# Relu and square of score tiles by single banks in half-sized buffers, with GpSimd ordered behind planned two-input DVE work and with measured durations in the plan

## Chip, cores and metric

One core of a Trainium2 chip. The metric is the device time of one execution in microseconds (us); a profile's span is 1.7 to 2.0 us shorter than the time of the same execution. Kernels are compared by runs taken in alternation on one chip. All profiles here are of state fast (the two with a single timed run: unknown), with a mean granted TensorE clock of 0.985 to 1.0.

## The reference

Attention with the square of relu in place of softmax, then a two-layer network with the same activation:

```python
scores = (q @ k.transpose(0, 1, 3, 2)) / sqrt(64)          # q, k, v: 8 x 12 x 448 x 64, fp32
attn = np.maximum(scores, 0.0) ** 2 / 448
x = (attn @ v).transpose(0, 2, 1, 3).reshape(3584, 768)
r = np.maximum(x @ w_in, 0.0)                               # w_in: 768 x 2048
out = (r * r) @ w_out                                       # w_out: 2048 x 768
```

## The kernel before

The kernel is planned before it is emitted: operations are added with their dependencies, buffers, due times and, for some, several engines to choose from; a list scheduler with a table of durations fixes engine, order and buffer of each, and then all are emitted in that order. So a change of a duration or of a buffer re-plans everything after it.

A score tile is two PSUM banks of 448 columns. Each bank is scaled and cut at zero by DVE or ACT into half of a wide fp32 buffer, and one instruction squares both halves, on ACT or GpSimd:

```python
"rel": fixed(sb, "rel", 4, [P, 1024], FP32),
...
first = [plan.add([dve(width, ...), act(width, ...)], [op], [sp[e], r], due=plan.now + 0.2)
         for e in range(2)]
second = plan.add([
    act(n, lambda: nc.scalar.activation(out=dst(), in_=rel(), func=AF.Square)),
    ("POOL", 0.0018 * n + 0.05, 0.0018 * n + 0.08,
     lambda: nc.gpsimd.tensor_mul(dst(), rel(), rel()))],
    first, [r, at], due=plan.now + 4.0)               # n = 2 * width
```

The output side multiplies sums of activations (and of the weights `w_out`) to save matmuls. These sums ("combinations") are two-input fp16 operations on DVE; the plan starts one only when GpSimd is free, or adds GpSimd's rest to its duration:

```python
st[name] = plan.add([("DVE", 0.6, 0.68, emit, 0, True)], deps, [buf] + srcs), buf
```

The emitted program had no order between the two engines there. GpSimd also issues the loads that cast to fp16, among them those of `v`, which the plan held as one operation of two transfers:

```python
for r in range(2):
    hs = slice(1, 3) if r else slice(0, 4, 3)
    nc.gpsimd.dma_start(out=buf.tile[64 * r:64 * r + 64], in_=src[:, u, hs])
```

In the first 45 us, where PE has nothing to do in the plan, filler matmuls are emitted.

## Time and profile before

| | before |
|---|---|
| time, median of 3 runs | 383.37 us (383.33 to 383.42) |
| the profiled run, and its span | 384.0 us, 382.0 us |
| PE busy | 371.8 us, 97% |
| DVE, ACT, GpSimd busy | 268.5, 272.0, 191.0 us |

The lines of the profile that carry the argument stand in the prediction; a line of a group gives operation, shapes and count, then busy us and mean ns of one, then the idle time before them and what ended it.

### The profile page before, as it was taken

The page shows a single profiled execution, that of the slowest core. Times are in us where ns is not written, and L with a number is a line of the kernel's source. Part 1 is how long each engine was busy: PE and PEld are TensorE (multiplying, and loading weights), DVE is VectorE, ACT ScalarE, POOL GpSimd, SP SyncE. Part 2 cuts the span into 40 slices and gives each one's busy share as a digit, 9 for nine tenths or more (in the row PEclk, how much of TensorE's full clock was granted, in tenths as well). Part 3 has the DMA queues.
Part 4 walks back from the last instruction along what each step waited for, and adds up shares of the span by engine and source line. Part 5 has one row for each costly group of instructions (what it writes and reads, how often), then busy time and mean ns, then how long its engine had stood idle before and what let it go on. Part 6 is the DMA issues. An engine that isn't in the chain of part 4 may idle for free.

```text
span 382.0 us, 8653 instructions
## 1 busy us (share of the span) xinstructions
PE 371.8 (97%) x3283; PEld 197.9 (52%) x3283; DVE 268.5 (70%) x464; ACT 272.0 (71%) x500; POOL 191.0 (50%) x184
## 2 busy tenths in 40 slices
PE   7799999999999999999999999999999999999995
PEld 3445565544465445544554555545555545555553
DVE  2976889687975677687996575885886768256731
ACT  4998999699877788687876786786794784244221
POOL 7987768383726665565564554664641333001000
PEclk9989999999999999999999999999999999999999
DMA  8999998987278966559369664674553002300243
GB/s 179 194 208 198 195 225 221 247 194 167 48 184 190 159 177 135 120 142 206 79 127 218 159 169 73 180 170 94 129 105 82 2 1 54 73 21 0 61 106 82
DMA packets 70216, 51.34 MB, mean 134 GB/s; under 512 B 36896, under 2 KB 70176, under 8 KB 70176
## 3 DMA queue, kind: packets, MB, share of 16 engines
q1 hardware_dynamic: 52384, 35.86, 38.2%
q0 software_dynamic: 16928, 14.09, 24.6%
q10 hardware_dynamic: 864, 0.85, 0.6%
q8 instruction: 25, 0.41, 0.4%
q14 instruction: 15, 0.12, 0.1%
HBM read 45.61 MB, written 11.01 MB: 148 GB/s over the span
## 4 chain that ended last, share of the span: by engine, by line
PE 92%; ACT 2%; DMA 2%; DVE 1%; POOL 1%; issue 1%; POOLq 0%; ACTq 0%
PE mm L632 38%; PE mm L846 31%; PE mm L505 10%; PE mm L570 8%; PE mm L781 3%; DMA g<-in_q_dram 2%; PE mm L681 2%; PE mm L444 1%; ACT comb L539 1%; DVE comb L825 1%; ACT rel L535 0%; POOL at L541 0%; DVE g L616 0%; ACT at L539 0%; PE mm L708 0%
## 5 line engine op out<-in xcount | busy, mean ns | idle before, releaser
L632 PE MATMUL mm<-xt,w 128*128 128x448 f16 (+1 forms) x768 | 149.0, 346 | 0.1
L541 POOL TENSOR_TENSOR at<-rel 128x896 f16<-128x896 f32 (+1 forms) x63 | 102.2, 1626 | 92.5 <-DVE rel L532 76.5
L616 DVE SCALAR_TENSOR_TENSOR g<-mm,g 128x448 f16<-128x448 f32 (+1 forms) x128 | 77.3, 605 | 50.4 <-ACT g L621 48.9
L632 PEld LDWEIGHTS <-w 128*128 128x128 f16 x768 | 72.3, 98 | 70.4 <-issue 11.7
L532 DVE TENSOR_SCALAR rel<-mm 128x448 f32<-128x448 f32 (+2 forms) x172 | 95.6, 596 | 15.7 <-PE mm L505 14.1
L621 ACT ACTIVATE g<-mm 128x448 f16<-128x448 f32 (+1 forms) x128 | 68.4, 539 | 47.2 <-PE mm L632 47.1
L539 ACT ACTIVATE at<-rel 128x896 f16<-128x896 f32 (+1 forms) x105 | 97.7, 948 | 1.1 <-DVE rel L532 0.6
L535 ACT ACTIVATE rel<-mm 128x448 f32<-128x448 f32 (+2 forms) x176 | 84.8, 550 | 2.9 <-PE mm L505 2.7
L846 PEld LDWEIGHTS <-comb 128*128 128x128 f16 x416 | 39.5, 98 | 30.3 <-issue 4.3
L765 ACT ACTIVATE part<-mm 128x384 f32<-128x384 f32 x45 | 22.3, 499 | 44.6 <-PE mm L846 42.3
L505 PE MATMUL mm<-qkt,qkt 64*64 64x448 f16 (+2 forms) x756 | 52.6, 340 | 1.4 <-DVE rel L532 0.3
L424 POOL CAST blk<-raw 128x896 f16<-128x896 f32 x36 | 36.5, 1024 | 23.4 <-DMA raw<-in_k_dram 11.7
L858 DVE SCALAR_TENSOR_TENSOR part<-mm,part 128x384 f32<-128x384 f32 x52 | 28.3, 554 | 24.9 <-ACT part L765 13.8
L846 PE MATMUL mm<-wt,comb 128*128 128x384 f16 x208 | 36.8, 327 | 0.2 <-DVE comb L825 0.2
L846 PE MATMUL mm<-w,comb 128*128 128x384 f16 x208 | 36.7, 327 | 0.0
L846 PEld LDWEIGHTS <-g 128*128 128x128 f16 x264 | 25.3, 98 | 19.1 <-issue 2.7
L570 PE MATMUL mm<-at,vs 64*64 64x448 f16 (+1 forms) x672 | 35.1, 344 | 0.0
L505 PEld LDWEIGHTS <-qkt 64*64 64x64 f16 x756 | 19.1, 106 | 26.2 <-issue 21.4
L474 POOL DMA_DIRECT2D vs<-in_v_dram x48 | 29.8, 631 | 4.2 <-DVE rel L532 2.0
L846 PE MATMUL mm<-w,g 128*128 128x384 f16 x176 | 31.1, 327 | 0.1
L570 PEld LDWEIGHTS <-vs 64*64 64x64 f16 x756 | 22.2, 108 | 14.7 <-issue 4.9
L747 POOL COPY rest<-g 128x1024 f16<-128x1024 f16 x8 | 8.8, 1103 | 40.6 <-DVE g L616 40.6
(61 smaller groups left out, 207.8 us busy)
## 6 DMA issues: line engine op xcount, KB each, us to landing
out_dram<-part SPq DMA_DIRECT2D x108, 96.0 KB, 2.2
raw<-in_k_dram SPq DMA_DIRECT2D x18, 448.0 KB, 4.2
raw<-in_q_dram SPq DMA_DIRECT2D x18, 448.0 KB, 5.0
vs<-in_v_dram POOLq DMA_DIRECT2D x48, 112.0 KB, 4.3
w<-in_moe_w_in_dram POOLq DMA_DIRECT2D x4, 768.0 KB, 11.8
w<-in_moe_w_out_dram POOLq DMA_DIRECT2D x4, 768.0 KB, 13.5
g<-in_k_dram POOLq DMA_DIRECT2D x4, 224.0 KB, 11.4
g<-in_q_dram POOLq DMA_DIRECT2D x4, 224.0 KB, 9.9
```

Of the source, the lines that this page charges most:

```text
L424: return lambda: fn(blk.tile.rearrange("p t (f d) -> p f t d", f=2), tile_of().rearrange("p f (t d) -> p f t d", d=D))
L474: nc.gpsimd.dma_start(out=buf.tile[64 * r:64 * r + 64], in_=src[:, u, hs])
L505: nc.tensor.matmul(sp[e].tile[64 * c:64 * c + 64, c0:c0 + w].rearrange("p (t c) -> p t c", c=TP), lhsT=kT[r, t, 64 * e:64 * e + 64], rhs=q ...
L532: dve(width, lambda e=e: nc.vector.tensor_scalar(out=rel()[:, e], in0=sp[e].tile[:, 0:width], scalar1=0.0, scalar2=SK, op0=ALU.max, op1=AL ...
L535: act(width, lambda e=e: nc.scalar.activation(out=rel()[:, e], in_=sp[e].tile[:, 0:width], func=AF.Relu, scale=SK))],
L539: act(n, lambda: nc.scalar.activation(out=dst(), in_=rel(), func=AF.Square)),
L541: lambda: nc.gpsimd.tensor_mul(dst(), rel(), rel()))],
L570: nc.tensor.matmul(banks[f].tile[64 * e:64 * e + 64, c0:c0 + w], lhsT=vs[r, e ^ c, t * D:(t + 1) * D], rhs=a[r, e, :], start=(t == 0), sto ...
L616: nc.vector.scalar_tensor_tensor(out=dst, in0=src, scalar=0.0, in1=dst, op0=ALU.is_gt, op1=ALU.mult)
L621: nc.scalar.activation(out=dst, in_=src, func=AF.Square)
L632: nc.tensor.matmul(bank.tile[:, c0:c0 + w], lhsT=w1[f // 4][:, m, f % 4 * P:(f % 4 + 1) * P], rhs=xts[b].tile[:, m, cols], start=(m == 0), ...
L846: nc.tensor.matmul(buf.tile[:, 0:HALF], lhsT=lhs()[:, j, :], rhs=w[:, j, :], start=(first and j == 0), stop=(j == NH - 1), skip_group_chec ...
```

## The change

Its intent: a square can start when one bank is ready, buffers come free in halves, the plan's durations are closer to the measured ones, the two transfers of `v` are planned one by one, and GpSimd's compute really waits where the plan had DVE's two-input work go first.

```diff
-        for emit in self.order:
-            emit()
+        alone = None
+        for emit, op in self.order:
+            got = emit()
+            if op is None:
+                continue
+            if len(op.way) > 5:
+                alone = got
+            elif alone is not None and op.engine == "POOL" and not op.size:
+                self.behind(got, alone)
+                alone = None
...
-                            self.sent += [op.end + (0.8 if op.end > 15.0 else 0.0)] * (2 if op.size == 458752 and took > 1.0 else 1)
+                            self.sent.append(op.end + (0.8 if op.end > 15.0 else 0.3))
...
-        "rel": fixed(sb, "rel", 4, [P, 1024], FP32),
+        "rel": fixed(sb, "rel", 8, [P, 512], FP32),
...
-        vst[n] = plan.add([("POOL", 1.25, 1.25, emit, QK)], bufs=[buf], after=after, due=due), buf
+        vst[n] = [plan.add([("POOL", 0.62, 0.62, emit(r), QK // 2)], bufs=[buf], after=after,
+                           due=due) for r in range(2)], buf
...
+        return plan.add([
+            act(width, lambda: nc.scalar.activation(
+                out=dst(), in_=r.tile[:, 0:width], func=AF.Square)),
+            ("POOL", 0.13 + 0.00172 * width, 0.19 + 0.00172 * width,
+             lambda: nc.gpsimd.tensor_mul(dst(), r.tile[:, 0:width], r.tile[:, 0:width]))],
+            [first], [r, at], due=plan.now + 4.0)
```

(`behind` adds a dependency of the GpSimd instruction on the DVE one. Cut: the rest of the new `squared`, and returns of instructions.)

More of the change, by code (lines that the diff above doesn't have):

```diff
@@ L205, in simulate @@
                         busy, took = busy + wait, took + wait
-                    op.engine, op.start = eng, begin
+                    op.engine, op.start, op.way = eng, begin, alt
                     op.end = begin + took
@@ L219, in simulate @@
                             b.tile, b.slot = slot[2], slot[1]
-                    self.order.append(emit)
+                    self.order.append((emit, op))
                     heapq.heappush(events, self.busy[eng])
@@ L259, in fill @@
             slot = min(free)
-            self.order.append(lambda: self.filler(slot[2]))
+            self.order.append((lambda: self.filler(slot[2]), None))
             self.pools["mm"].remove(slot)
@@ L348, with behind @@
     plan.cold = 6.6
+    def behind(later, first):
+        tc.add_manual_dep(
+            later.ins, first.ins.name, mybir.DependencyInfo(
+                mybir.DependencyClass.Sync, mybir.DependencyReason.ANTI), reason="shared port")
+    plan.behind = behind
     def act(n, emit):
@@ L469, in load_v, with emit @@
         src = v[b].rearrange("(u x) (p t) d -> p u x (t d)", x=4, t=TJ)
-        def emit():
-            for r in range(2):
-                hs = slice(1, 3) if r else slice(0, 4, 3)
-                nc.gpsimd.dma_start(out=buf.tile[64 * r:64 * r + 64], in_=src[:, u, hs])
-        vst[n] = plan.add([("POOL", 1.25, 1.25, emit, QK)], bufs=[buf], after=after, due=due), buf
+        def emit(r):
+            hs = slice(1, 3) if r else slice(0, 4, 3)
+            return lambda: nc.gpsimd.dma_start(
+                out=buf.tile[64 * r:64 * r + 64], in_=src[:, u, hs])
+        vst[n] = [plan.add([("POOL", 0.62, 0.62, emit(r), QK // 2)], bufs=[buf], after=after,
+                           due=due) for r in range(2)], buf
     def load_w1(i, after, due=None):
@@ L515, in scores, with squared, dst @@
                        "tile", at)
-    def square(op, sp, width, pool="at"):
-        at, r = Buf(pool), Buf("rel")
-        flat = [2, width]
-        def rel():
-            return r.tile[:, 0:2 * width].rearrange("p (e c) -> p e c", e=2)
-        def dst():
+    def squared(op, bank, width, dst, at):
+        r = Buf("rel")
+        first = plan.add([
+            dve(width, lambda: nc.vector.tensor_scalar(
+                out=r.tile[:, 0:width], in0=bank.tile[:, 0:width], scalar1=0.0, scalar2=SK,
+                op0=ALU.max, op1=ALU.mult)),
+            act(width, lambda: nc.scalar.activation(
+                out=r.tile[:, 0:width], in_=bank.tile[:, 0:width], func=AF.Relu, scale=SK))],
+            [op], [bank, r], due=plan.now + 0.2)
+        return plan.add([
+            act(width, lambda: nc.scalar.activation(
+                out=dst(), in_=r.tile[:, 0:width], func=AF.Square)),
+            ("POOL", 0.13 + 0.00172 * width, 0.19 + 0.00172 * width,
+             lambda: nc.gpsimd.tensor_mul(dst(), r.tile[:, 0:width], r.tile[:, 0:width]))],
+            [first], [r, at], due=plan.now + 4.0)
+    def square(op, sp, width, pool="at"):
+        at = Buf(pool)
+        def dst(e):
             t = at.tile
@@ L527, in dst @@
                 t = t.rearrange("p f c -> p (f c)").rearrange("p (e c) -> p e c", e=2)
-            return t[:, :, 0:width]
-        n = 2 * width
-        first = [plan.add([
-            dve(width, lambda e=e: nc.vector.tensor_scalar(
-                out=rel()[:, e], in0=sp[e].tile[:, 0:width], scalar1=0.0, scalar2=SK,
-                op0=ALU.max, op1=ALU.mult)),
-            act(width, lambda e=e: nc.scalar.activation(
-                out=rel()[:, e], in_=sp[e].tile[:, 0:width], func=AF.Relu, scale=SK))],
-            [op], [sp[e], r], due=plan.now + 0.2) for e in range(2)]
-        second = plan.add([
-            act(n, lambda: nc.scalar.activation(out=dst(), in_=rel(), func=AF.Square)),
-            ("POOL", 0.0018 * n + 0.05, 0.0018 * n + 0.08,
-             lambda: nc.gpsimd.tensor_mul(dst(), rel(), rel()))],
-            first, [r, at], due=plan.now + 4.0)
-        return second, at
+            return t[:, e, 0:width]
+        return [squared(op, sp[e], width, lambda e=e: dst(e), at)
+                for e in range(2)], at
     xts: dict = {}
@@ L576, in av @@
         before = av_ops.get(n, [])[-1:] + (av_ops[n - 1][-1:] if joint else [])
-        op = plan.pe(max(0.1, 0.000437 * w) * len(ts), emit, [z[0] for z in used] + [vst[n][0]] + before,
+        op = plan.pe(max(0.1, 0.000437 * w) * len(ts), emit, [y for z in used for y in z[0]] + vst[n][0] + before,
                      [z[1] for z in used] + [vst[n][1]] + banks, "tile", at)
@@ L746, in emit @@
             def emit(i=i, b=b):
-                nc.gpsimd.tensor_copy(buf.tile[:, :, 64 * i:64 * i + 64],
-                                      gts[b].tile[:, :, 3 * P:S])
+                return nc.gpsimd.tensor_copy(buf.tile[:, :, 64 * i:64 * i + 64],
+                                             gts[b].tile[:, :, 3 * P:S])
             ops.append(plan.add([("POOL", 1.55, 1.6, emit)], g_ops[b], [buf, gts[b]]))
@@ L824, in emit @@
             def emit():
-                fn(buf.tile, x(), y())
+                return fn(buf.tile, x(), y())
             st[name] = plan.add([("DVE", 0.6, 0.68, emit, 0, True)], deps, [buf] + srcs), buf
```

## The prediction

> **What bounds the kernel now.** I read the page first, then busy time by stretch, the waits of the matmul engine, its timeline around the end of the start-up, and the groups by shape. The page's totals and chain:
>
> ```profile
> PE 371.8 (97%) x3283; PEld 197.9 (52%) x3283; DVE 268.5 (70%) x464; ACT 272.0 (71%) x500; POOL 191.0 (50%) x184
> PE 92%; ACT 2%; DMA 2%; DVE 1%; POOL 1%; issue 1%; POOLq 0%; ACTq 0%
> ```
>
> TensorE is busy for 97% of the span and holds 92% of the chain that ended last. Busy time by stretch tells where the rest is:
>
> ```profile
> 10.00:20.00 10.00, 7.62 (x213) 5.07 (x213) 9.12 (x22) 9.89 (x16) 9.46 (x13) 0.95 1.22 196
> 20.00:32.00 12.00, 11.27 (x140) 5.69 (x133) 8.67 (x20) 11.48 (x26) 9.12 (x9) 0.90 1.24 205
> ...
> 100.00:340.00 240.00, 240.00 (x1950) 125.37 (x1948) 172.79 (x290) 172.83 (x317) 117.41 (x102) 1.00 0.54 122
> 340.00:378.00 38.00, 37.60 (x222) 21.36 (x220) 20.64 (x35) 11.27 (x22) 1.56 (x1) 1.00 0.21 50
> ```
>
> The columns after the stretch's length are PE, PEld, DVE, ACT, POOL, then the granted clock, the DMA share and GB/s. From 100 to 340 us PE has no idle time at full clock, while DVE and ACT have 28% to spare. Only before 32 us is it the other way round: ACT is nearly full and PE waits. After 36 us, the waits of PE's matmuls hold one row:
>
> ```profile
> PE mm L846 <- DVE comb L825: 0.2, 1, 0.2
> ```
>
> A wait that the pipeline's modelled ends hide would not show there, so I also compared the spacing of matmul starts with its usual value for the shape. After 36 us I found some 1.3 us of excess in all, the largest 0.33 us at 353.7 us. So the relus and squares are off the path after the start-up.
>
> What ends the start-up is visible in PE's timeline and in the rows of the load of the first weight:
>
> ```profile
> 31.33 0.32 PE L505 MATMUL mm<-qkt,qkt 64*64 64x320 f16 x2 [0.29 <-DVE xt L592]
> 31.84 0.27 PE L991 MATMUL mm<-part 128*128 128x256 f16 x1 [0.19 <-ACT xt L590]
> 31.95 1.46 PE L681 MATMUL mm<-w,xt 128*128 128x512 f16 x6
> ```
>
> ```profile
> L479 POOL DMA_DIRECT2D w<-in_moe_w_in_dram x4: 828/840/887, 10.7 to 14.4; - x4
> ...
> DMA to landing us min/median/max: 8.6/11.8/17.4
> ```
>
> The last quarter of the weight is issued at 14.42 us and takes 17.4 us, the maximum of the row: it lands at 31.83 us. The fourth L681 block, the first to use it, starts at 31.95 us after one filler (L991). I call this start the gate. PE does useful tile work before it, waits and fillers included, but the same matmuls must run after it.
>
> **What the Trainium skill says.** SBUF — State Buffer, section "Who interferes with whom": a DVE operation with two SBUF inputs contends with GpSimd's reads, and the one that issues second fully blocks. The trace agrees: the two-input L825 takes 0.68 us alone, and next to a GpSimd copy it takes 1.52 us (excerpt below); I count 12 of 52 that were stretched, by 8.6 us together, the worst to 2.38 us. TensorEngine Tiling (Array Packing), section "Key Properties": changing the tiling mode drains TensorE. The trace agrees, with the cost worked out below. DMA: Bandwidth & Descriptors, section "SWDGE vs HWDGE vs iDMA": only one context is allocated for DMAs that GpSimd issues, and casts must go there. The trace fits one line of transfers: landings come in issue order, and the DMA share is above 1.2 from 10 to 60 us. GPSIMD Engine Reference, section "3.1 Elementwise — side-by-side cycle accounting": some 2.6 cycles per element for two inputs. Here the slope is smaller, next part.
>
> **The change part by part.** First, squares in halves. Before:
>
> ```profile
> L541 POOL TENSOR_TENSOR at<-rel 128x896 f16<-128x896 f32 x54 | 91.0, 1686 | 91.3 <-DVE rel L532 75.3 <-ACT rel L535 8.5 <-PE mm L570 5.3
> L539 ACT ACTIVATE at<-rel 128x896 f16<-128x896 f32 x93 | 88.9, 973 | 1.0 <-DVE rel L532 0.6 <-ACT g L621 0.2
> L541 POOL TENSOR_TENSOR at<-rel 128x640 f16<-128x640 f32 x9 | 11.2, 1263 | 1.3 <-DVE rel L532 1.2
> L541 POOL TENSOR_TENSOR comb<-rel 128x256 f16<-128x256 f32 x1 | 0.7, 657 | 0.0
> ```
>
> On GpSimd the slope is (1686 - 657) / 640 = 1.61 ns a column (1.9 cycles at the 1.2 GHz of the skill's table), with about 245 ns fixed; 448 columns should take 0.97 us, so two halves cost 1.93 us for 1.69 us. On ACT, 448 columns to fp16 take 0.55 us in another group (the evacuation to xt), two of them 1.10 us for 0.97 us, but the work is about equal because more moves to GpSimd. From the order of the built program: ACT gets 166 halves of 448 where it had 93 wholes, GpSimd 128 where it had 54 wholes, and one of the weight combinations as well. Estimates by engine: GpSimd 128 x 0.97 + 16 x 0.76 + 3 x 1.07 + 0.9 + 3 for the combination = 143 us for 103 us, so 191 goes to about 230 us (60%). ACT 166 x 0.55 + 26 x 0.45 + 7 x 0.60 = 107 us for 103 us, less three relus and three part copies, 3 us: about 273 us. DVE gains those, about 3 us, and loses contention. All of it lies beside PE's 240 us of full work, so on the path it costs about nothing.
>
> Second, GpSimd waits behind DVE's planned two-input work. It takes back most of the 8.6 us of stretch on L825 and 1.2 us on L810: DVE about 262 us. On the path it is worth one place, at the end:
>
> ```profile
> 351.39 0.69 DVE L825 TENSOR_TENSOR comb<-g 128x1024 f16<-128x1024 f16 x1
> 352.00 1.52 DVE L825 TENSOR_TENSOR comb<-g,g 128x1024 f16<-128x1024 f16 x1
> 353.45 0.68 DVE L825 TENSOR_TENSOR comb<-comb,g 128x1024 f16<-128x1024 f16 x1
> ```
>
> ```profile
> 351.42 1.56 POOL L747 COPY rest<-g 128x1024 f16<-128x1024 f16 x1 [30.82 <-DVE g L616]
> ```
>
> The GpSimd copy blocks the second combination by 0.84 us, and PE then waits for the third one, 0.33 us by spacing. With the copy behind, that wait goes: -0.3 us. The copy itself is needed only at 355.1 us.
>
> Third, the measured durations change the order of everything. Counted in the built program, TensorE has the same 2,862 matmuls from the gate on, before and after, but 56 changes from dense to tiled matmuls and 56 back where it had 59 and 59. One pair, from the timeline:
>
> ```profile
> 202.68 0.73 PE L632 MATMUL mm<-xt,w 128*128 128x448 f16 x3
> 203.34 0.57 PE L505 MATMUL mm<-qkt,qkt 64*64 64x448 f16 x8
> 203.85 1.31 PE L632 MATMUL mm<-xt,w 128*128 128x448 f16 x6
> ```
>
> Three dense matmuls at their usual 0.189 us are 0.57 us and took 0.66; eight scores, four at a time at 0.179 us, are 0.36 us and took 0.51. A pair costs about 0.24 us, and three fewer give -0.7 us.
>
> Before the gate the work is the same too, but fillers go from 8 to 20. Fifteen stand in early waits for loads. Five stand just before the gate where there was one, at 0.11 us each. If PE comes there early, they are free; if it comes only when the weight lands, they cost up to 0.4 us. Four scores fewer are left between the third AV burst and the gate, so PE should come earlier; I put +0.2 us. The DMAs issued by GpSimd stay in the same order, with squares among them; the second quarter of the weight was issued 6.5 us before the first one landed (12.73 and 19.28 us), so 1 us of delay there leaves the line full and the gate in place.
>
> New waits from new places of halves I put at +0.3 us, a quarter of the present excess. Sum: -0.7 - 0.3 + 0.2 + 0.3 = -0.5 us; 383.4 becomes 382.9 us.
>
> **The rivals.** (1) The start-up shortens: ACT is 99% busy from 10 to 20 us, halves are ready sooner and GpSimd takes more, so PE could gain 2 to 4 us of its idle time there: 380 to 381 us. For it speaks the chain, which goes through squares between 11 and 19 us; against it the landing at 31.83 us, which no relu moves. (2) GpSimd becomes a bound: its squares come late for AV, as it has 20% more to do and now waits for DVE too. A few waits of 0.3 to 1 us would make 384 to 386 us. Against it speak 76.5 us in which its squares waited for DVE's relus, so it is short of input, not of time. (3) Delayed issues: a square waiting on DVE in GpSimd's order holds back a load and empties the line, so the gate slips by 1 to 2 us: 384 to 385 us. The slack of 6.5 us speaks against it. (4) The landing itself falls differently: the last quarter came 4.94 us after the third where the others were 3.8 us apart. If that goes, up to 1 us is gained.
>
> **Range and chances.** All certain terms are under 1 us; the landing and the new waits give the width, a little more on the slower side for (2) and (3). 8 in 10: 381.6 to 384.2 us. A change of 2% is 7.7 us, and PE idles for only 10.2 us in the whole span (382.0 - 371.8). Faster by over 2%: 0.02; within: 0.96; slower: 0.02.
>
> **What would show it.** Right: the fourth weight block starts at 31.9 to 32.4 us; PE has no idle time from 100 to 340 us; L825 near 0.68 us with few above 1; GpSimd near 230 us; PE's last matmul some 345.1 us after the gate, where it now ends 345.8 us after it (377.8 - 31.95). Wrong: a gate more than 1 us away, which would make rival (1), (3) or (4) the truth; or PE waits for at or rel after 60 us, rival (2).

## The result, and the profile after

The changed kernel took 382.85 us (median of 4, 382.81 to 383.00), the kernel before in the same rounds 383.35 us. The ratio of the fast runs is 0.9989, with a 95% interval of 0.9972 to 1.0006. A ratio here is the mean time of one kernel's fast runs over that of the other's in the same rounds, so it is not quite the ratio of the medians. By this measurement alone the sign is not settled.

Totals and chain of the changed kernel:

```profile
PE 372.0 (98%) x3295; PEld 198.6 (52%) x3295; DVE 267.0 (70%) x468; ACT 269.8 (71%) x584; POOL 221.4 (58%) x270
PE 85%; DMA 9%; POOL 3%; ACT 1%; issue 1%; DVE 0%; DVEq 0%
```

GpSimd has 30 us more to do, and the chain holds DMA for 9%: a part of it now runs through transfers. Busy time by stretch (PE, PEld, DVE, ACT, POOL, clock, DMA share, GB/s), with 60 to 100 us, where PE loses 0.5 us:

```profile
10.00:20.00 10.00, 8.05 (x223) 5.28 (x216) 9.56 (x21) 9.91 (x26) 9.62 (x14) 1.00 1.22 193
20.00:32.00 12.00, 10.99 (x134) 5.72 (x133) 9.93 (x22) 11.96 (x35) 11.94 (x19) 1.00 1.25 206
...
60.00:100.00 40.00, 39.50 (x333) 20.20 (x332) 30.67 (x52) 35.28 (x77) 30.52 (x35) 1.00 0.82 169
100.00:340.00 240.00, 240.00 (x1950) 124.40 (x1949) 170.65 (x293) 170.30 (x364) 135.39 (x155) 1.00 0.55 123
```

The gate, in PE's timeline (L1009 are the fillers, L699 the fourth block of the first weight), and the load's source rows (last issue at 14.2 us, 16.6 us to its landing):

```profile
30.40 0.98 PE L1009 MATMUL mm<-part 128*128 128x256 f16 x5
31.22 1.46 PE L699 MATMUL mm<-w,xt 128*128 128x512 f16 x6
```

```profile
L496 POOL DMA_DIRECT2D w<-in_moe_w_in_dram x4: 826/846/887, 10.3 to 14.2; - x4
...
DMA to landing us min/median/max: 9.1/12.4/16.6
```

The weight landed at 30.84 us by the trace, 1 us earlier than in the profile of before, and the gate came 0.38 us after it, behind fillers. ACT's last evacuation to xt before the gate (L608) ended at 31.06 us; that this, and not the landing, sets the gate here is shown below. The groups of squares:

```profile
L548 POOL TENSOR_TENSOR at<-rel 128x448 f16<-128x448 f32 x128 | 119.1, 949 | 67.6 <-DVE rel L538 50.6 <-ACT rel L541 8.4 <-DVE comb L843 5.8
L545 ACT ACTIVATE at<-rel 128x448 f16<-128x448 f32 x166 | 90.4, 601 | 0.5 <-PE mm L588 0.5
```

DVE and GpSimd near the end, where before a copy stretched a combination to 1.52 us:

```profile
350.81 0.69 DVE L843 TENSOR_TENSOR comb<-g 128x1024 f16<-128x1024 f16 x1
351.42 0.68 DVE L843 TENSOR_TENSOR comb<-g,g 128x1024 f16<-128x1024 f16 x1
352.02 0.68 DVE L843 TENSOR_TENSOR comb<-comb,g 128x1024 f16<-128x1024 f16 x1
```

```profile
352.77 1.04 POOL L765 COPY rest<-g 128x1024 f16<-128x1024 f16 x1 [31.82 <-DVE comb L843]
```

The copy begins behind the third combination and ends PE's wait of before. The waits of PE's matmuls after 36 us:

```profile
PE mm L522 <- DMA qkt<-blk: 0.4, 1, 0.4
PE mm L522 <- DVE rel L538: 0.2, 1, 0.2
```

The first is new: a score at 75.2 us waits for a transposed load of q or k. By the spacing of starts it costs 0.55 us.

Two lengths are used from here on. "Gate lag" is the time from the landing of the last quarter of the first weight to the gate. "After the gate" is the time from the gate to the start of the last matmul; all kernels have the same 2,862 matmuls in it, but for e9 and e10, with three fillers more each, and e11 and e12, with the 16 that were added. "Stall" is the excess of one spacing over its usual value, listed from 55 ns on.

### The profile page after: what moved, and what is told of

Read it like the earlier page. It is cut to its first block, busy times and chain, and to the rows that moved or that the text cites. A ratio compares the mean times of both kernels' runs of the same rounds, so it can differ in the third digit from the quotient of the medians.

```text
span 381.1 us, 8809 instructions
## 1 busy us (share of the span) xinstructions
PE 372.0 (98%) x3295; PEld 198.6 (52%) x3295; DVE 267.0 (70%) x468; ACT 269.8 (71%) x584; POOL 221.4 (58%) x270
## 4 chain that ended last, share of the span: by engine, by line
PE 85%; DMA 9%; POOL 3%; ACT 1%; issue 1%; DVE 0%; DVEq 0%
PE mm L650 34%; PE mm L864 32%; PE mm L522 8%; PE mm L588 7%; DMA w<-in_moe_w_out_dram 5%; DMA vs<-in_v_dram 3%; PE mm L799 2%; POOL at L548 2%; DMA qkt<-blk 2%; PE mm L1006 1%; PE mm L460 1%; POOL g L406 1%; PE mm L1009 1%; ACT rel L541 0%; ACT comb L545 0%
## 5 line engine op out<-in xcount | busy, mean ns | idle before, releaser
L548 POOL TENSOR_TENSOR at<-rel 128x448 f16<-128x448 f32 (+1 forms) x144 | 130.1, 924 | 67.7 <-DVE rel L538 50.6
L538 DVE TENSOR_SCALAR rel<-mm 128x448 f32<-128x448 f32 (+3 forms) x176 | 97.6, 596 | 14.6 <-PE mm L522 13.2
L545 ACT ACTIVATE at<-rel 128x448 f16<-128x448 f32 (+1 forms) x192 | 101.5, 589 | 0.5 <-PE mm L588 0.5
L541 ACT ACTIVATE rel<-mm 128x448 f32<-128x448 f32 (+2 forms) x172 | 83.0, 548 | 5.4 <-PE mm L522 5.1
L783 ACT ACTIVATE part<-mm 128x384 f32<-128x384 f32 x42 | 20.9, 497 | 44.0 <-PE mm L864 43.1
L440 POOL CAST blk<-raw 128x896 f16<-128x896 f32 x36 | 33.5, 945 | 21.8 <-DVE wt L828 5.4
```

The source lines that it names most:

```text
L440: return lambda: fn(blk.tile.rearrange("p t (f d) -> p f t d", f=2), tile_of().rearrange("p f (t d) -> p f t d", d=D))
L538: dve(width, lambda: nc.vector.tensor_scalar(out=r.tile[:, 0:width], in0=bank.tile[:, 0:width], scalar1=0.0, scalar2=SK, op0=ALU.max, op1= ...
L541: act(width, lambda: nc.scalar.activation(out=r.tile[:, 0:width], in_=bank.tile[:, 0:width], func=AF.Relu, scale=SK))],
L545: act(width, lambda: nc.scalar.activation(out=dst(), in_=r.tile[:, 0:width], func=AF.Square)),
L548: lambda: nc.gpsimd.tensor_mul(dst(), r.tile[:, 0:width], r.tile[:, 0:width]))],
```

## The experiments

Twelve kernels ran, in three calls; each call has its own runs of the kernel before (medians 383.32, 382.97 and 383.31 us). There the runs of the kernel before spread over 1.6 to 2.6 us, so intervals are wide, and the lengths from the traces say more than medians. Of the eight ways to combine the change's three parts (halves, split loads, waits), halves with the waits alone was not run.

**e1, control: the kernel before again, no edit.** It asks whether the earlier gate belongs to the change.

> The kernel before, run once more for a second profile. In the two profiles at hand the fourth block of the first weight (the gate) starts at 31.95 us before and at 31.22 us after, because the last quarter of the weight landed at 31.83 and 30.84 us. Theory A (my prediction: the change does not move the landing, it differs from run to run): this profile's gate lies away from 31.95 us, by 0.3 us or more earlier, and the span is 381.4 us or less; the profile of before was its slow one (384.0 us against a median of 383.4). Theory B (the change moves the gate): gate again at 31.9 to 32.0 us. Ratio 1.000.

PE's timeline at the gate:

```profile
30.71 0.27 PE L991 MATMUL mm<-part 128*128 128x256 f16 x1 [0.19 <-ACT xt L590]
30.82 1.46 PE L681 MATMUL mm<-w,xt 128*128 128x512 f16 x6
```

The gate is at 30.82 us, not 31.95, in a span of 380.8 us; the landing was at 30.69 us. The same program moved its gate by 1.1 us, as Theory A had it. That the landing moved it does not follow: the third weight block came 1.1 us earlier too (26.96 us for 28.10), and in the first profile that block began 1.21 us after its own quarter had landed. After the gate it took 345.45 us, against 345.49 in the first profile, with the same stalls. So after the gate a kernel repeats to 0.04 us here, and the gate does not. Over the two first profiles and those of e1 to e10 the landing lay between 30.45 and 32.46 us. Time 382.97 us, ratio 0.9991 (0.9962 to 1.0019).

**e2, the change without the waits behind DVE work.**

```diff
-                self.behind(got, alone)
```

> The changed kernel without the waits of GpSimd behind two-input DVE work; all orders are those of the changed kernel. Theory A (the waits give back 0.33 us at the end, where a GpSimd copy stretched a combination, and cost 0.5 us at 74.8 us, where the casts of q and k wait up to 4.4 us for the weights' combinations and a transposed load comes late): the stall of 0.55 us at 74.8 us is gone or under 0.2 us, a stall of about 0.3 us comes back at 353 us, and the time is 382.6 to 382.9 us, no worse than the change. Theory B (the waits are a gain throughout): 383.2 us or more. Either way some ten or more of the 52 combinations take over 0.85 us.

```profile
PE mm L863 <- DVE comb L842: 0.5, 2, 0.3
```

```profile
100.41 1.52 DVE L842 TENSOR_TENSOR comb<-g,g 128x1024 f16<-128x1024 f16 x1
```

```profile
99.88 1.50 POOL L764 COPY rest<-g 128x1024 f16<-128x1024 f16 x1
```

The three are a row of PE's waits after 36 us, where a combination now ends two of them, and a line each of DVE's and GpSimd's timelines: a copy beside which a combination takes 1.52 us, as at the end of the kernel before. 383.75 us, ratio 1.0021 (0.9980 to 1.0063; one of the six runs took 388.51 us); after the gate 346.27 us, against 345.29 for the change. The stalls that Theory A named did as it said: the one at 74 us was gone and 0.32 us came back at 354.2 us. The first is no proof, since e4 and e5 lack that stall with the waits in place. On the sum it was wrong: matched matmul by matmul with the change, it had missed 0.47 us at 102 us, 0.61 at 195 and 0.17 at 282.5 us. Sixteen of 52 combinations took over 0.85 us, against 8 with the waits. With halves on GpSimd and split loads the waits are worth 1.0 us after the gate against the first profile of the change, and 1.6 us against that of e5 (344.67 us).

**e3, the kernel before with the waits alone.** The edit adds the loop with `behind` from the diff and nothing else.

> The kernel before with the waits of GpSimd behind two-input DVE work and nothing else; no order changes. Theory A: the stall of 0.33 us at 353.7 us goes, something of up to 0.3 us comes at 60 to 90 us, where GpSimd casts wait behind the weights' combinations; 383.0 to 383.4 us. Theory B (removing 8.6 us of stretch on DVE shortens the kernel): 382.5 us or less. Combinations over 1 us: five or fewer of 52.

DVE's timeline near the end:

```profile
351.63 0.68 DVE L841 TENSOR_TENSOR comb<-g,g 128x1024 f16<-128x1024 f16 x1
352.23 0.68 DVE L841 TENSOR_TENSOR comb<-comb,g 128x1024 f16<-128x1024 f16 x1
353.30 1.26 DVE L841 TENSOR_TENSOR comb<-g,comb 128x1024 f16<-128x1024 f16 x1
```

After the gate 345.11 us, 0.34 less than the control, and the only stall that differs by more than 10 ns is the one of 0.33 us at the end, which is gone. This is the tail term by itself. 383.00 us, ratio 0.9984 (0.9956 to 1.0012). Nine combinations still took over 1 us, where I had expected five: the dependency holds GpSimd work that stands later in the plan, not work that is running when DVE gets there. The fourth combination above, 1.26 us, meets the copy that was moved. The gate stood 0.57 us after the landing (31.61 and 31.04 us), with one filler before it, and that filler had waited for ACT:

```profile
31.50 0.27 PE L1007 MATMUL mm<-part 128*128 128x256 f16 x1 [0.20 <-ACT xt L606]
31.61 1.46 PE L697 MATMUL mm<-w,xt 128*128 128x512 f16 x6
```

**e4, the change without the fillers just before the gate.**

```diff
+        count[0] += 1
+        if count[0] <= 15:
             nc.tensor.matmul(bank[:, 0:256], ...)
```

> The changed kernel without the five filler matmuls just before the gate. In the profile of the changed kernel the weight landed at 30.84 us and the gate came at 31.22 us, behind fillers that began at 30.40 us. Theory A (fillers delay the gate when the weight comes early): gate within 0.15 us of the landing, 382.85 minus 0.2 to 0.3, so 382.6 us. Rival (the gate waits for something else there, or the clock falls without fillers): no gain, 382.85 us or more.

PE's timeline at the gate:

```profile
30.33 0.44 PE L522 MATMUL mm<-qkt,qkt 64*64 64x320 f16 x8
31.59 1.47 PE L699 MATMUL mm<-w,xt 128*128 128x512 f16 x6 [0.82 <-DMA w<-in_moe_w_in_dram]
```

PE now waits for the weight itself: landing 31.54 us, gate lag 0.05 us instead of 0.38. But the landing was late here, after ACT's last evacuation to xt (31.37 us), and the gate stands later than in the first profile of the change, not earlier. So this lag does not show that the fillers cost 0.3 us; e7 says more. After the gate 344.63 us. 382.55 us, ratio 0.9971 (0.9946 to 0.9996): the only interval below 1. This is the version that beats the kernel before; it was not run beside the change, and that it beats the change by 0.3 us is not shown.

**e5, the changed kernel again.**

> The changed kernel once more, for a second profile and five more rounds: the control run showed that the landing before the gate differs by 1 us from run to run, so the 0.5 us between the medians may be chance. Theory A (the change gives 0.2 us from the gate to the end and loses up to 0.4 us at the gate by fillers): ratio 0.999 to 1.001; from the gate to the last matmul 345.1 to 345.4 us; the gate 0.1 to 0.5 us after the landing. Theory B (the 0.5 us of the first measurement is real and comes from the start): ratio 0.9985 or less and a gate before 31.2 us.

382.66 us against 382.97 us, ratio 0.9985 (0.9967 to 1.0004). Gate 30.77 us, lag 0.32 us: as Theory A. After the gate 344.67 us, shorter than it gave: the stall at 74.5 us and one of 0.15 us at 40.9 us are absent here, the others are as in the first profile. So the change runs in two ways after the gate, about 344.7 and 345.3 us. Theory B's early gate came too, with early landings (the last at 30.45 us); but the control had its gate at 30.82 us with no change at all, which rules its reading out.

**e6, no waits behind the combinations of weights.** In the changed kernel GpSimd's casts of q and k wait for those; from the waits of GpSimd from 56 to 76 us, in all, times and longest:

```profile
POOL blk L440 <- DVE wt L828: 5.4, 2, 4.4
```

```diff
-            if len(op.way) > 5:
+            if len(op.way) > 5 and op.way[1] < 0.7:
```

> The changed kernel, but GpSimd waits only behind the combinations of activations, not behind those of the weights near 60 to 75 us. Theory A (the wait of 4.4 us of the casts of q and k behind the weights' combinations makes the stall of 0.55 us at 74.5 us): that stall falls under 0.2 us, the casts run near 61 to 62 us instead of 66 us, and the path from the gate to the end is 0.3 to 0.5 us shorter than that of the changed kernel (345.3 us): 344.8 to 345.0 us. Rival (the stall hangs on when the second weight lands, not on the wait: the run without the last fillers had no such stall): no difference to the second run of the changed kernel.

From the timelines of DVE and GpSimd in e6:

```profile
74.28 4.99 DVE L828 TENSOR_TENSOR w<-w,w 128x1536 f16<-128x1536 f16 x1
```

```profile
75.31 3.13 POOL L825 TENSOR_TENSOR w<-w,w 128x1536 f16<-128x1536 f16 x1
```

The stall at 74.5 us went, but a new one of 1.53 us came at 78 us: without the order, the two engines' weight combinations met, DVE's took 4.99 us instead of 1.0, and the relus behind it held back PE's scores. After the gate 347.21 us in a profiled run of 384.74 us. The timed runs split: four at 381.78 to 382.50, two at 383.96 and 384.74 us; median 382.39, ratio 0.9994 (0.9970 to 1.0018). In the profiled run, one of the two slow ones, my expectation failed, and the wait would have protected more than it costs. The four quicker runs, below the 382.66 us of e5, have no profile, so whether the wait pays on the whole is not shown. Whether it also causes the stall at 74.5 us stays open, since that stall is absent in e4 and e5, where the wait is in place.

**e7, early issue.** The change without late fillers, and the first two loads of GpSimd ahead of the making of the identity.

```diff
-    make_identity(nc, ident)
 ...                                  # loads of the first two
+    make_identity(nc, ident)
```

> The changed kernel without the five last fillers, and with the first two loads that GpSimd issues moved ahead of the making of the identity, so that the line of transfers starts about 0.7 us earlier (0.75 instead of 1.47 us). If the landing of the last quarter of the first weight sets the gate: landing and gate 0.5 to 0.7 us earlier than in runs with the same luck, gate near 30.3 us, 382.0 us. Rival (the early line is limited by the shared transfers of the first q and k, or PE is not ready then): gate unchanged at 30.8 to 31.6 us, 382.6 us as without the fillers.

PE's timeline at the gate:

```profile
31.41 1.46 PE L709 MATMUL mm<-w,xt 128*128 128x512 f16 x6 [0.98 <-ACT xt L618]
```

No gain: landing at 31.20 us, gate 31.41 us, 382.69 us, ratio 0.9986 (0.9964 to 1.0009). With no filler in the way the gate waited for ACT's evacuation to xt, which ended at 31.35 us, and not for the weight. The first cast load landed at 6.80 us, some 0.6 us earlier than in e5 (7.41), and by the first quarter of the weight the lead was lost: 19.79 us against 18.65. In several profiles one quarter takes 0.4 to 1.2 us longer than the usual 3.8 us, the fourth in the first profile of before, the second in e1; I have no explanation. A stall of 0.87 us stood at 74.5 us.

**e8, halves alone.** The kernel before with the new `squared`, eight half buffers and the new durations.

> The kernel before with the squares by single banks in half-sized buffers and their durations, without the waits behind DVE work and without the splitting of the loads of v in the plan. The built order has 55 pairs of mode changes from the gate on (before 59, change 56) and 3 fillers just before the gate. Theory A (a pair is worth about 0.24 us, contention takes it back when nothing holds GpSimd back): pairs give 1.0 us, stalls of 1 us or more come where combinations are stretched; gate to end 345.3 to 346.0 us, 383.2 to 383.8 us. Theory B (finer squares are a gain in themselves): gate to end under 345.0 us and 382.7 us or less.

PE's waits after 36 us, and the timeline around the longest:

```profile
PE mm L847 <- DVE comb L826: 1.5, 2, 1.3
```

```profile
148.65 3.34 DVE L826 TENSOR_TENSOR comb<-comb,g 128x1024 f16<-128x1024 f16 x1
148.63 1.82 POOL L424 CAST blk<-raw 128x896 f16<-128x896 f32 x2
150.39 1.05 POOL L748 COPY rest<-g 128x1024 f16<-128x1024 f16 x1
```

386.83 us, ratio 1.0091 (1.0070 to 1.0111): slower by 3.5 us, by the ratio. After the gate 348.84 us. A combination that began 0.02 us after a GpSimd cast was passed by two casts and a copy before it could end, and PE waited 1.47 us by spacing. At 33.3 to 36.2 us a burst of 28 AV matmuls, which waited for late GpSimd squares, took 2.94 us instead of the usual 1.07. Finer squares are no gain in themselves; Theory B is out, and Theory A underrated the loss.

**e9, the split loads alone, and e10, the split loads with the waits behind DVE work** (so e10 is the change without the halves). The edits are those lines of the diff.

> The kernel before with only the loads of v split in the plan and the plan's count of pending transfers changed: whole squares, no waits behind DVE work. The order has 55 and 56 mode changes from the gate on (before 59 and 59). Theory A (orders matter by pairs of mode changes at 0.24 us, less new stalls): gate to end 0.5 us or more shorter than before's 345.45 us if stalls stay near 1.1 us; 382.5 to 383.0 us. Rival (the plan without the measured durations sends GpSimd and DVE into each other more, as in the run with halves alone): stalls of 2 us or more, 384 us or more.

> The kernel before with the split loads and the waits behind DVE work, so the change without the halves. Theory A (halves are not what gains; pairs and the waits are): gate to end 344.3 to 344.9 us, equal to the changed kernel's 344.7 us or shorter, no late fillers, so 382.2 to 382.6 us, no worse than the change. Rival (halves matter): gate to end longer than 345.2 us and 383.0 us or more.

PE's timeline in e10, and a piece of its chain (start, us, what):

```profile
75.07 0.38 PE L522 MATMUL mm<-qkt,qkt 64*64 64x448 f16 x4
80.34 0.59 PE L522 MATMUL mm<-qkt,qkt 64*64 64x448 f16 x4 [4.89 <-DMA qkt<-blk]
```

```profile
69.82 10.39 DMA qkt<-blk
```

391.27 and 390.16 us (e10 has one slow run; its five fast ones have a median of 389.92), ratios 1.0205 (1.0173 to 1.0238) and 1.0155 (1.0112 to 1.0198): the worst of all. The rivals' ranges (384 us or more, 383.0 us or more) hold, but no theory of mine had the main cause. In both the score at 75 to 76 us waits for a transposed load, 2.6 us by spacing in e9 and 5.1 us in e10; the load took 10.4 us to land in e10 where it took 6.3 us in the change. It is the spot at which the change stalls for 0 to 0.9 us. In e9 a combination of 4.32 us at 150.6 us adds a stall of 1.85 us. Half a microsecond before these waits ended PE's clock fell as well (at 78.53 us in e9, 79.81 in e10); e10, the stretch after the wait, with columns as above (clock third from the end):

```profile
80.30:83.30 3.00, 2.96 (x11) 1.21 (x12) 2.27 (x3) 0.54 (x1) 2.99 (x2) 0.51 1.06 211
```

The mean granted clock of the 3 us after the wait is 0.51, and dense matmuls start every 0.373 us for a while, not every 0.189.

**e11 and e12, the cost of a change of mode.** The kernel before, with one extra matmul of 64 columns ahead of each of the 16 groups of the last dense stretch: 64x64 (tiled) in e11, 128x128 (dense) in e12. The group overwrites its bank, and the results are correct.

```diff
+            if b == B - 1:
+                nc.tensor.matmul(bank.tile[0:64, 0:64], lhsT=w1[0][0:64, 0, 0:64],
+                                 rhs=w1[0][0:64, 0, 64:128], start=True, stop=True, ...)
             for m in range(NM):
```

> The kernel before with one extra 64x64 matmul of 64 columns, tiled mode, at the head of each of the 16 groups of six dense matmuls from 331 to 350 us, where nothing else is on PE; it writes a bank that the group then overwrites, so the result is unchanged. Each adds one pair of mode changes. Theory A (a pair costs about 0.2 us besides the work): the stretch of 96 dense matmuls grows from 18.2 us by 16 x (0.2 + 0.03) = 3.7 us, to some 21.9 us. Rival (the three pairs are worth under 0.1 us each and the gain came from elsewhere): under 20.2 us.

> The same with the extra matmul dense, 128x128 weights and 64 columns, so with no change of mode: its control. Theory A: 16 x 0.03 to 0.06 us, so 18.7 to 19.2 us for the stretch; the difference to the tiled run, over 16, is the cost of a pair: 0.15 to 0.25 us. Rival: the extra matmul alone costs as much as in the tiled run.

The first group in the chains of e11, e12 and, for the stretch without additions, e1:

```profile
331.00 0.14 PE mm L632
331.14 1.24 PE mm L634 x6
```

```profile
330.74 0.03 PE mm L632
330.76 1.13 PE mm L634 x6
```

```profile
330.79 18.17 PE mm L632 x96
```

The stretch took 22.16 us tiled (331.00 to 353.16), 18.64 us dense (330.74 to 349.38), 18.17 us without. The dense addition costs 0.03 us each; the tiled one (22.16 - 18.64) / 16 = 0.22 us more. That is a pair of mode changes, as Theory A had it.

## Why the prediction was right

The time came out as forecast, 382.9 for 382.85 us, and a part of this exactness is luck: gates and fast runs spread by more than the whole effect, and by its interval the ratio does not even settle the sign. The terms of its sum, one by one, from the clean pair e5 and e1:

| term | predicted | measured |
|---|---|---|
| three pairs of mode changes | -0.7 | 3 x 0.22 = -0.66 (e11, e12) |
| combination at the end | -0.3 | -0.34 (e3) |
| fillers at the gate | +0.2 | about 0 (both gates 0.16 us after ACT, see below) |
| new stalls | +0.3 | +0.28 (e5); +0.97 in the first profile |
| sum | -0.5 | -0.7 to 0.0; medians -0.50 and -0.31 |

The gates of that pair lie 0.05 us apart (30.77 and 30.82 us). After the gate the difference is 344.67 - 345.45 = -0.78 us, and the listed stalls are 1.08 us in e5 against 1.13 us, or 0.80 in e1 without the one at the end: hence the +0.28. What is left, -0.78 + 0.34 - 0.28 = -0.72 us, is what the order gave, against 0.66 us from the dummies.

Right: that the relus and squares are off the path from 100 to 340 us (PE busy for 240.00 us of 240 before and after), and that the waits pay at one place on the path.

Wrong: "the landing at 31.83 us, which no relu moves", as what sets the gate. From the traces, in us:

| | third block | its quarter landed | ACT's last xt done | last quarter landed | gate |
|---|---|---|---|---|---|
| before | 28.10 | 26.89 | 31.79 | 31.83 | 31.95 |
| e1, before again | 26.96 | 26.89 | 30.66 | 30.69 | 30.82 |
| e3, before with waits | 27.76 | 27.21 | 31.45 | 31.04 | 31.61 |
| e12, before, dense addition | 26.89 | 26.37 | 30.58 | 30.17 | 30.74 |
| change | 27.65 | 27.61 | 31.06 | 30.84 | 31.22 |
| e5, change again | 26.88 | 26.65 | 30.61 | 30.45 | 30.77 |
| e7, change, no late filler | 27.62 | 27.40 | 31.35 | 31.20 | 31.41 |

With the start-up of the kernel before, which is the same in its two profiles and in e3, e11 and e12, the gate comes 3.85 us after the third block and 0.16 us after ACT's last evacuation to xt each time, while its lag behind the landing varies from 0.12 to 0.57 us. PE's own order of work and ACT set it; the landing was near by coincidence. The line of the filler in the prediction says so: [0.19 <-ACT xt L590]. The change's gate with five fillers comes 0.16 us after ACT as well, so four more fillers cost nothing to be seen; e7, without one, has about 0.05 us. Only where the weight landed more than 0.1 us after ACT was done (e4, e8, e9, e10) does the gate follow the landing, by 0.04 to 0.05 us.

Rival (1) is therefore half right. In the six profiles with the change's start-up (change, e2, e4 to e7) the first weight block starts at 18.94 to 19.84 us, against 20.73 to 21.60 us in the five of before. But then its first three blocks start, with one exception of 0.62 us, within 0.3 us of the landing of their quarter, so the loads now limit it, and the gates of the two groups are the same in the mean, 31.2 us. The gain of 2 to 4 us did not come; e1 has as early a gate as e5 with no change at all. Whether halves, split loads or the 15 early fillers brought the earlier start was not tested. Rival (4), a luckier landing, is not what moved the gate between the first two profiles, and the gate that the prediction gave as its sign (31.9 to 32.4 us) did not come: 31.22 us.

One rival stands untested. In four of the five start-ups of before PE's clock was at half for 3.41 us (19.10 to 22.51 us in the first profile), and in none of the six of the change. Thirteen of the 33 runs of before in the rounds of the experiments have a mean clock of 0.995 or less; in the first two calls these were slower in the mean than the rest by 1.2 and 0.7 us, in the third quicker by 0.3. So a part of the difference of medians may come from the clock.

Right in kind, wrong in size: DVE was to fall to 262 us and is 267.0. "It takes back most of the 8.6 us of stretch on L825" is the term that was mis-sized: 4.5 us of stretch are left, because the waits hold only GpSimd work that comes later in the plan. GpSimd came to 221 and not 230 us: a half takes 0.95 us in the mean as forecast for 0.97, but instructions that follow each other overlap by some 0.06 us. The squares of ACT take 0.60 us each, not 0.55.

Incomplete: the prediction gave each part its own small cost, as if parts added up. They do not. Halves alone lose 3.5 us, split loads 8 us, split loads with waits 6 us; e2, halves with split loads, loses 0.8 us by the ratio. Halves and split loads each re-plan the whole, and what counts is how the built order falls at two weak spots: a combination that GpSimd passes by, and the transposed load needed at 75 us. Rival (3) had seen that order can hold a load back, but looked at the gate alone, and "new waits" was a guess at a quarter of the present excess that happened to fit. Why the split loads alone make the transposed load so late is not settled: it is issued only 1.1 us later than in the change (69.8 us in e10, 68.7 us there), and then takes 4 us longer among other transfers. That a different mix of transfers does it is argued, not shown.

## What to carry to other kernels

Where PE is full, look for what its order costs (here 0.22 us for a pair of mode changes) and for what gates it; freeing engines beside it moved nothing here. A transfer that lands just before a wait ends need not have ended it: see over several profiles which of two events keeps its distance. Before explaining 1 us, profile the unchanged kernel a second time and measure from a fixed event, because the length after the gate repeated to 0.04 us while the gate moved by 1.1. In a planned kernel, judge a change by the order that it builds: parts that are harmful alone can be neutral together.

## What the Trainium skill lacked or had wrong

- TensorEngine Tiling (Array Packing), section "Key Properties", says that a change of mode drains TensorE but gives no cost. A pair of changes cost 0.22 us here (e11 less e12, over 16).
- SBUF — State Buffer, section "Who interferes with whom": the one that issues second fully blocks for the whole of the other's instruction. A combination can lose several times in a row: 3.34 us in e8 against 0.68 alone, while two casts and a copy of GpSimd went by; 4.99 us in e6, where it started 1.0 us before GpSimd's combination (and 0.2 us after GpSimd had begun to issue loads).
- TensorE: Matmul & The Clock Gate, section "HAM oscillation — how this bites in real kernels", gives as a rule no PE idle gaps over about 3.4 us. In e9 the clock fell 1.9 us into a wait of 2.4 us, to half for 3.41 us; in the first profile of before it fell at 19.10 us, with no gap over 0.7 us in the 10 us before.
- GPSIMD Engine Reference, section "3.1 Elementwise — side-by-side cycle accounting": 2.6 cycles an element for two inputs. For fp32 inputs that are one and the same tensor and an fp16 output the slope was 1.61 ns a column, 1.9 cycles at that page's clock.
- DMA: Bandwidth & Descriptors, section "DMA Transpose (X-bar)", says nothing of how long one takes beside other traffic. Here it took 3 us in quiet places and 5.8 to 10.4 us at 68 to 70 us.
